# A fused attention and expert kernel: the first chunk's instructions in another order, 16 constant matmuls behind the first scores, ranks one tile later

## The chip, the cores and the metric

The kernel runs on one core of a Trainium2 chip. The metric is device time in microseconds of one execution; lower is better. TensorE (PE) does the matmuls, VectorE (DVE), ScalarE (ACT) and GpSimd (POOL) the elementwise work, SyncE (SP) issues most transfers.

## The reference

Three stages in a row: a linear attention with a decaying state, a choice of one expert for each token, and a gated feed-forward layer.

```python
B, H, S, D = 4, 8, 768, 48
for t in range(S):                                   # attention, by batch and head
    cur = einsum('bhd,bhe->bhde', u * k[t], v[t])
    y[t] = einsum('bhd,bhde->bhe', r[t], state + cur)
    state = w * state + einsum('bhd,bhe->bhde', k[t], v[t])
x = y as (3072, 384)
logits = x @ w_gate                                  # experts, 8 of them
e = argmax(logits); gate = softmax(logits)[e]; eom = sigmoid(x @ w_output_gate)[e]
x = gate * eom * (relu(x @ w1[e]) @ w2[e])
xn = x / sqrt(mean(x * x) + 1e-6) * rms_g            # feed-forward, 1536 wide
out = (silu(xn @ w_gate2) * (xn @ w_val)) @ w_out
```

## The kernel before

The attention works on 24 tiles of 128 tokens: six chunks of the sequence, in each of them the four batches. Inside a tile the recurrence is a product of r and k (by feature, `rkTb`), each multiplied by powers of w (`decayT`), under a triangular mask; from tile to tile a state `st[b]` is carried. A tile n goes through these steps:

- `decayT(n)`: VectorE multiplies the transposed r and k by the table of powers. `decayk(n)` does the same for k by token (VectorE for n < 2, GpSimd later).
- `product(n)`, `sums(n)`, `weigh(n)`: GpSimd forms r u k, VectorE sums it by head, ScalarE weighs v with it. This is the diagonal term `qv`.
- `scores(n)`: TensorE's 8 matmuls into two PSUM banks `pa` (L322), then two masks on VectorE (L324). Both buffers of the pool are used by one tile, so the next tile's scores need the masks of this one done.
- `attend(n, between)`: products of the masked scores with v into `px`, eight matmuls of 48 columns (L343) in two halves of four; in the first chunk the diagonal term is added behind them (L346, 384 columns), in later chunks it is added ahead of them (L333), with the product of r and the state (L335). Then the state's matmuls into `pkv` (L360, and L358 in later chunks) and VectorE's multiplication (L363).
- `xtrans(n)` transposes the row of outputs (L372), ScalarE copies it (L375), `logits(n)` multiplies it with the gates' weights (L383, 16 columns). `between` is called inside `attend` and holds the logits of the tile before.
- `route` works on the logits of a whole chunk. It is a generator with `yield`s, and `advance()` takes one piece of it in each tile: VectorE's choice and running counts (to L434), TensorE's ranks `prk` (L439, L440), VectorE's positions and gates (L459 to L479). `send` scatters the rows, one or two in a tile from tile 10 on.

`busy(ps, m)` issues m matmuls of constants, 128 x 512, whose result nobody reads. The table that gives their number at each place:

```python
NBUSY = (16, 8, 10, 3, 1, 1, 8)
NFILL = 6
```

TensorE, VectorE and ScalarE execute in the order in which the code is written; the order on GpSimd and SyncE is set by a scheduler, which also places the waits. The loop over n calls the steps of several tiles: with `attend(n)` come `scores(n + 1)`, `decayT(n + 2)`, `product(n + 3)` and the load of tile n + 4.

Of the kernel before, what the change touches and what calls it, by code (L numbers as in the profile page):

```python
# [39 lines left out]
NBUSY = (16, 8, 10, 3, 1, 1, 8)  # L40
# [11 lines left out]
def fused_kernel(  # L52
# [130 lines left out]
    with tc.tile_pool(name="at1", bufs=1) as at1, \  # L183
# [130 lines left out]
        def scores(n):  # L314
# [3 lines left out]
            busy(pas[0].rearrange("p a n -> p (a n)"), NBUSY[3] if n == NT - 1 else NBUSY[6] if n == 1 else NBUSY[4] if n < NFILL else 0)  # L318
# [6 lines left out]
            am[n] = a.rearrange("p g j t -> p (g j) t")  # L325

        def attend(n, between):
# [9 lines left out]
            between()  # L337
            if c < NCH - 1:
                pkv = ps1.tile([P, 512], F32, tag="kv", name=f"pkv_{n}")
            for h in range(H):  # L340
                if h == H // 2 and n < NFILL:
                    busy(pkv, NBUSY[5])
                nc.tensor.matmul(px[:, h * D:(h + 1) * D], am[n][:, h, :], vv[:, h * D:(h + 1) * D],  # L343
                                 start=(c == 0 and h == 0), stop=(c > 0), skip_group_check=True)
            if c == 0:
                nc.tensor.matmul(px[:, :DM], ident, qv.pop(n), start=False, stop=True, skip_group_check=True)  # L346
            if 1 < n + 1 < NT:
                weigh(n + 1)
            if b == 0:
# [3 lines left out]
            if c < NCH - 1:  # L353
                s = st[b] if c > 0 else at1.tile([PP, G, PD], F32, name=f"s{b}")
                sf = s.rearrange("p g e -> p (g e)")
                if c > 0:

                    nc.tensor.matmul(pkv[:PP, :DM], ident[:PP, :PP], sf, start=True, stop=False, skip_group_check=True)  # L358
                for g in range(G):
                    nc.tensor.matmul(pkv[:PP, g * PD:(g + 1) * PD],  # L360
                                     kd[n].rearrange("p h d -> p (h d)")[:, g * 2 * HP:g * 2 * HP + PP],
                                     vv[:, g * PD:(g + 1) * PD], start=(c == 0), stop=True, skip_group_check=True)
                nc.vector.tensor_tensor(sf, pkv[:PP, :DM], w128.rearrange("p g e -> p (g e)"), op=ALU.mult)  # L363
                st[b] = s
# [26 lines left out]
        def route(c, b0, b1):  # L391
# [43 lines left out]
            yield  # L435

# [81 lines left out]
        decayT(1)  # L518
# [6 lines left out]
        scores(0)  # L525

        nc.vector.tensor_tensor(pw[:, 7, :], pw[:, 6, :], pw[:, 6, :], op=ALU.mult)
        w128 = at1.tile([PP, G, PD], F32, name="w128")
# [7 lines left out]
        nc.vector.memset(cum, 0.0)  # L536

        for n in range(-3, NT + 1):
# [4 lines left out]
            if 0 <= n + 3 < NT:  # L543
                if n != -2:
# [4 lines left out]
            if n == 0:  # L549
                decayT(n + 2)  # L550
# [615 lines left out]
```

## Time and profile before

| | us |
|---|---|
| median of three runs | 923.24 |
| lowest, highest | 922.04, 928.17 |
| profiled execution | 925.68 |
| its span, first to last instruction | 923.9 |
| TensorE busy in it | 892.5 (97%) |
| mean granted clock of TensorE | 0.972 of full speed |

The span is 1.8 us shorter than the time of the same execution. A line of the timeline gives the start, the time, the engine, the line of the code, the operation with its tiles and shapes, the number of instructions that it merges, and in brackets the idle time of that engine before it with what ended it. Matmuls of 32-bit data are recorded twice, so eight of them read x16.

### The profile page before, as it was taken

The page shows a single profiled execution, that of the slowest core. Times are in us where ns is not written, and L with a number is a line of the kernel's source. Part 1 is how long each engine was busy: PE and PEld are TensorE (multiplying, and loading weights), DVE is VectorE, ACT ScalarE, POOL GpSimd, SP SyncE. Part 2 cuts the span into 40 slices and gives each one's busy share as a digit, 9 for nine tenths or more (in the row PEclk, how much of TensorE's full clock was granted, in tenths as well). Part 3 has the DMA queues.
Part 4 walks back from the last instruction along what each step waited for, and adds up shares of the span by engine and source line. Part 5 has one row for each costly group of instructions (what it writes and reads, how often), then busy time and mean ns, then how long its engine had stood idle before and what let it go on. Part 6 is the DMA issues. An engine that isn't in the chain of part 4 may idle for free.

```text
span 923.9 us, 12722 instructions
## 1 busy us (share of the span) xinstructions
PE 892.5 (97%) x4912; PEld 783.3 (85%) x4912; DVE 505.1 (55%) x887; ACT 350.8 (38%) x742; POOL 278.5 (30%) x250
## 2 busy tenths in 40 slices
PE   7899999979999999999999999999999999999997
PEld 4788888848999999998878778888888888888886
DVE  6457798755677777877579843422432242233102
ACT  1435546544444544455443422322322142241211
POOL 6446697630000000103312132132123123124121
PEclk8789979988999999999999999999999999999999
DMA  6579866444675566533321000000000000000000
GB/s 181 156 234 284 252 198 198 137 154 131 203 244 180 188 203 209 178 126 104 137 69 50 19 35 1 1 16 19 0 1 35 1 1 35 1 0 35 1 1 34
DMA packets 34263, 93.55 MB, mean 101 GB/s; under 512 B 4368, under 2 KB 12584, under 8 KB 34200
## 3 DMA queue, kind: packets, MB, share of 16 engines
q1 hardware_dynamic: 23976, 53.53, 18.9%
q0 software_dynamic: 8928, 33.83, 11.4%
q10 hardware_dynamic: 1296, 5.35, 1.5%
q8 instruction: 39, 0.64, 0.3%
q14 instruction: 24, 0.20, 0.1%
HBM read 73.19 MB, written 19.50 MB: 100 GB/s over the span
## 4 chain that ended last, share of the span: by engine, by line
PE 80%; DVE 9%; issue 4%; ACT 3%; DMA 2%; POOL 1%; SPq 0%; POOLq 0%; DVEq 0%; ACTq 0%
PE ph L955 11%; PE px L343 5%; PE p2o L619 4%; PE p2o L617 4%; PE p2o L618 4%; PE pg L618 4%; PE pv L619 4%; PE pv L617 4%; PE pv L618 4%; PE pg L619 4%; PE pg L617 4%; PE po L617 4%; PE po L618 4%; PE po L619 4%; PE pa L322 3%
## 5 line engine op out<-in xcount | busy, mean ns | idle before, releaser
L1061 POOL TENSOR_TENSOR l<-sg,h 128x512 fp32r<-128x512 f32 x69 | 92.2, 1336 | 305.2 <-ACT h L1060 303.8
L1051 DVE TENSOR_TENSOR sg<-sg,pv 128x512 f32<-128x512 f32 x72 | 49.4, 686 | 236.7 <-PE pv L619 224.2
L619 PE MATMUL p2o<-hi_o,l 128*128 128x384 f32 x276 | 93.4, 338 | 3.2 <-POOL l L1061 3.2
L1050 ACT ACTIVATE sg<-pg 128x512 f32<-128x512 f32 x72 | 42.9, 596 | 139.7 <-PE pg L619 137.4
L617 PE MATMUL p2o<-hi_o,h 128*128 128x384 f32 x276 | 93.2, 338 | 1.3 <-ACT h L1060 1.3
L618 PE MATMUL p2o<-lo_o,h 128*128 128x384 f32 x276 | 92.7, 336 | 0.0
L1060 ACT CAST h<-sg 128x512 fp32r<-128x512 f32 x69 | 42.9, 621 | 130.7 <-DVE sg L1051 130.7
L617 PE MATMUL pv<-nh,hi_v 128*128 128x512 f32 x216 | 85.3, 395 | 0.9 <-ACT sg L1050 0.9
L618 PE MATMUL pg<-nl,hi_g 128*128 128x512 f32 x216 | 85.1, 394 | 0.5 <-DVE nl L904 0.5
L619 PE MATMUL pv<-nh,lo_v 128*128 128x512 f32 x216 | 85.2, 395 | 0.0
L618 PE MATMUL pv<-nl,hi_v 128*128 128x512 f32 x216 | 85.2, 395 | 0.0
L617 PE MATMUL pg<-nh,hi_g 128*128 128x512 f32 x216 | 85.2, 394 | 0.0
L619 PE MATMUL pg<-nh,lo_g 128*128 128x512 f32 x216 | 85.1, 394 | 0.0
L120 POOL DMA_DIRECT2D raw_w<-in_w_dram x25 | 19.0, 760 | 180.9 <-DVE hl L957 83.7
L955 PE MATMUL ph<-xh,hi_w 128*128 128x432 f32 x192 | 70.3, 366 | 1.8 <-DVE hl L957 1.4
L955 PE MATMUL ph<-xh,lo_w 128*128 128x432 f32 x192 | 69.8, 364 | 0.0
L955 PE MATMUL ph<-xl,hi_w 128*128 128x432 f32 x192 | 69.5, 364 | 0.0
L617 PE MATMUL po<-hh,hi_w 128*128 128x432 f32 x192 | 69.5, 362 | 0.0
L619 PE MATMUL po<-hh,lo_w 128*128 128x432 f32 x192 | 68.8, 358 | 0.0
L618 PE MATMUL po<-hl,hi_w 128*128 128x432 f32 x192 | 68.8, 358 | 0.0
L137 DVE TENSOR_TENSOR lo_w<-raw_w,hi_w 128x768 fp32r<-128x768 f32 x54 | 49.3, 955 | 19.9 <-ACT hi_w L133 19.9
L617 PEld LDWEIGHTS p2o<-hi_o,h 128*128 128x128 f32 x276 | 51.8, 188 | 5.3 <-ACT h L1060 2.1
(208 smaller groups left out, 1890.7 us busy)
## 6 DMA issues: line engine op xcount, KB each, us to landing
raw_w<-in_w_dram POOLq DMA_DIRECT2D x25, 768.0 KB, 5.4
rkTb<-in_rkt_dram SPq DMA_DIRECT2D x48, 192.0 KB
rk<-in_rkv_dram SPq DMA_DIRECT2D x24, 384.0 KB
raw_w<-in_w_dram SPq DMA_DIRECT2D x7, 768.0 KB
xs<-zt ACTq DMA_DIRECT2D x6, 770.0 KB
v<-in_rkv_dram SPq DMA_DIRECT2D x24, 192.0 KB
craw_g<-in_m2g_dram SPq DMA_DIRECT2D x9, 512.0 KB
craw_v<-in_m2v_dram SPq DMA_DIRECT2D x9, 512.0 KB
```

What stands on the lines that cost most here:

```text
L120: ld = self.queue.dma_start(raw.rearrange("p (a n) -> p a n", a=src.shape[1]), src)
L137: eng.tensor_tensor(lo[:, t], raw[:, t], hi[:, t].bitcast(F32), op=ALU.subtract)
L322: nc.tensor.matmul(pas[j][:, g, :], kT[n][t, g, :], rT[n][t, g, :], start=True, stop=True)
L343: nc.tensor.matmul(px[:, h * D:(h + 1) * D], am[n][:, h, :], vv[:, h * D:(h + 1) * D], start=(c == 0 and h == 0), stop=(c > 0), skip_group ...
L617: nc.tensor.matmul(ps, a[0], b[0], start=first, stop=False)
L618: nc.tensor.matmul(ps, a[0], b[1], start=False, stop=False)
L619: nc.tensor.matmul(ps, a[1], b[0], start=False, stop=last)
L955: nc.tensor.matmul(ph[:, :CAP], wp[:, o:o + P], xp[:, i, :CAP], start=(j == 0), stop=(j == len(parts) - 1))
L1050: nc.scalar.activation(sg, pg, AF.Silu)
L1051: nc.vector.tensor_tensor(sg, sg, pv, op=ALU.mult)
L1060: nc.scalar.copy(hh, sg)
L1061: (nc.vector if kept else nc.gpsimd).tensor_tensor(hl, sg, hh.bitcast(F32), op=ALU.subtract)
```

## The change

At the head, tile 0's masks and tile 0's decayed k go ahead of tile 1's decay on VectorE, and the constants that stood ahead of the scores of tiles 0 and 1 become 16 constant matmuls behind the scores of tile 0. In the first chunk `between`, with the logits of the tile before, moves from ahead of the products with v to between their two halves. Tile 0's state matmuls go ahead of its diagonal term; the transposes of tile 0 go ahead of tile 2's scores, with four constant matmuls behind them. In `route` the ranks of the first four chunks come one tile later by another `yield`. The rest of the diff moves the state's steps into a function of their own.

```diff
@@ -37,7 +37,7 @@
 
 
 
-NBUSY = (16, 8, 10, 3, 1, 1, 8)
+NBUSY = (16, 8, 10, 3, 1, 1, 16, 4)
 NFILL = 6
 NCOL = NTOK + CAP
 LEAST = 1.125 * 2.0 ** -15
@@ -315,7 +315,7 @@
 
             a = at2.tile([P, G, 2, P], F32, tag="am", name=f"am_{n}")
             pas = [ps2.tile([P, G, P], F32, tag="at", name=f"pa_{n}_{j}") for j in range(2)]
-            busy(pas[0].rearrange("p a n -> p (a n)"), NBUSY[3] if n == NT - 1 else NBUSY[6] if n == 1 else NBUSY[4] if n < NFILL else 0)
+            busy(pas[0].rearrange("p a n -> p (a n)"), NBUSY[3] if n == NT - 1 else NBUSY[4] if 1 < n < NFILL else 0)
             for g in range(G):
                 for j in range(2):
                     t = slice(j * HP, j * HP + D)
@@ -324,6 +324,23 @@
                 nc.vector.tensor_tensor(a[:, :, j, :], pas[j], bcast(smask.unsqueeze(1), [P, G, P]), op=ALU.mult)
             am[n] = a.rearrange("p g j t -> p (g j) t")
 
+        pkvs = {}
+
+        def state(n):
+            c, b = divmod(n, B)
+            vv, pkv = vin[n], pkvs.pop(n)
+            s = st[b] if c > 0 else at1.tile([PP, G, PD], F32, name=f"s{b}")
+            sf = s.rearrange("p g e -> p (g e)")
+            if c > 0:
+
+                nc.tensor.matmul(pkv[:PP, :DM], ident[:PP, :PP], sf, start=True, stop=False, skip_group_check=True)
+            for g in range(G):
+                nc.tensor.matmul(pkv[:PP, g * PD:(g + 1) * PD],
+                                 kd[n].rearrange("p h d -> p (h d)")[:, g * 2 * HP:g * 2 * HP + PP],
+                                 vv[:, g * PD:(g + 1) * PD], start=(c == 0), stop=True, skip_group_check=True)
+            nc.vector.tensor_tensor(sf, pkv[:PP, :DM], w128.rearrange("p g e -> p (g e)"), op=ALU.mult)
+            st[b] = s
+
         def attend(n, between):
             c, b = divmod(n, B)
             vv = vin[n]
@@ -334,34 +351,30 @@
                 for g in range(G):
                     nc.tensor.matmul(px[:, g * PD:(g + 1) * PD], rT[n][:, g, :], st[b][:, g, :],
                                      start=False, stop=False, skip_group_check=True)
-            between()
+            if c > 0:
+                between()
             if c < NCH - 1:
-                pkv = ps1.tile([P, 512], F32, tag="kv", name=f"pkv_{n}")
+                pkv = pkvs[n] = ps1.tile([P, 512], F32, tag="kv", name=f"pkv_{n}")
             for h in range(H):
                 if h == H // 2 and n < NFILL:
                     busy(pkv, NBUSY[5])
+                if h == H // 2 and c == 0:
+                    between()
                 nc.tensor.matmul(px[:, h * D:(h + 1) * D], am[n][:, h, :], vv[:, h * D:(h + 1) * D],
                                  start=(c == 0 and h == 0), stop=(c > 0), skip_group_check=True)
-            if c == 0:
+            if c == 0 and n > 0:
                 nc.tensor.matmul(px[:, :DM], ident, qv.pop(n), start=False, stop=True, skip_group_check=True)
             if 1 < n + 1 < NT:
                 weigh(n + 1)
+            if n == 0:
+                state(n)
+                nc.tensor.matmul(px[:, :DM], ident, qv.pop(n), start=False, stop=True, skip_group_check=True)
             if b == 0:
                 xt[c] = unit("xu", f"x_{c}").rearrange("p (b d) -> p b d", b=B)
                 nc.scalar.copy(xt[c][:, :, DM:], tokid[:, c * B:(c + 1) * B].unsqueeze(2))
             nc.scalar.copy(xt[c][:, b, :DM], px[:, :DM])
-            if c < NCH - 1:
-                s = st[b] if c > 0 else at1.tile([PP, G, PD], F32, name=f"s{b}")
-                sf = s.rearrange("p g e -> p (g e)")
-                if c > 0:
-
-                    nc.tensor.matmul(pkv[:PP, :DM], ident[:PP, :PP], sf, start=True, stop=False, skip_group_check=True)
-                for g in range(G):
-                    nc.tensor.matmul(pkv[:PP, g * PD:(g + 1) * PD],
-                                     kd[n].rearrange("p h d -> p (h d)")[:, g * 2 * HP:g * 2 * HP + PP],
-                                     vv[:, g * PD:(g + 1) * PD], start=(c == 0), stop=True, skip_group_check=True)
-                nc.vector.tensor_tensor(sf, pkv[:PP, :DM], w128.rearrange("p g e -> p (g e)"), op=ALU.mult)
-                st[b] = s
+            if 0 < n < NT - B:
+                state(n)
 
         xTt = {}
 
@@ -433,6 +446,8 @@
             tk = tokid[:, n0:n0 + nb]
             V.tensor_tensor(m2, m2, tk, op=ALU.subtract)
             yield
+            if n0 < NT - 2 * B:
+                yield
 
             pr = ps1.tile([P, 512], F32, tag="sm", name=f"prk_{n0}")
             prb = pr[:, :nb * E].rearrange("p (b e) -> p b e", b=nb)
@@ -515,16 +530,16 @@
         first = decayT(0)
         loadT(2)
         loadT(3)
-        decayT(1)
         pt = ps2.tile([P, 512], F32, tag="xT", name="pt")
         for g in range(G):
             nc.tensor.transpose(pt[:, g * PP:(g + 1) * PP], fw[:, g, :], ident[:PP, :PP])
         for j in range(2):
             nc.scalar.copy(ftab.rearrange("p (g j) d -> p g j d", g=G)[:, :, j, :],
                            pt[:, :G * PP].rearrange("p (g d) -> p g d", g=G)[:, :, j * HP:j * HP + D])
+
+        nc.vector.tensor_tensor(pw[:, 7, :], pw[:, 6, :], pw[:, 6, :], op=ALU.mult)
         scores(0)
-
-        nc.vector.tensor_tensor(pw[:, 7, :], pw[:, 6, :], pw[:, 6, :], op=ALU.mult)
+        busy(ps1.tile([P, 512], F32, tag="sm", name="busy2"), NBUSY[6])
         w128 = at1.tile([PP, G, PD], F32, name="w128")
         for j in range(2):
             nc.vector.tensor_tensor(w128[:, :, j * D:(j + 1) * D],
@@ -534,6 +549,8 @@
         nc.vector.tensor_scalar(iota8, rowi[:, 0:E], -1.0, float(E), op0=ALU.mult, op1=ALU.add)
         cum = at1.tile([P, E], BF16, name="cum0")
         nc.vector.memset(cum, 0.0)
+        decayk(0)
+        decayT(1)
 
         for n in range(-3, NT + 1):
             if 0 < n + 4 < NT and n + 4 > 1:
@@ -541,16 +558,22 @@
 
             late = NT - 3 <= n < NT
             if 0 <= n + 3 < NT:
-                if n != -2:
+                if n >= -1:
                     decayk(n + 3)
                 product(n + 3)
             if n == -2:
                 sums(0)
-            if n == 0:
-                decayT(n + 2)
+            if n == 1:
+                xtrans(0)
+                weigh(1)
+                busy(ps1.tile([P, 512], F32, tag="sm", name="busy3"), NBUSY[7])
             if 0 < n + 1 < NT:
                 scores(n + 1)
-            if 0 <= n - 1 and not late:
+            if n == 0:
+                sums(1)
+                decayk(1)
+                decayT(n + 2)
+            if 1 <= n - 1 and not late:
                 xtrans(n - 1)
             if 2 < n + 2 < NT:
                 decayT(n + 2)
@@ -574,10 +597,6 @@
                 xtrans(n - 1)
             if late or n not in range(NT):
                 route_on()
-            if n == 0:
-                sums(1)
-                weigh(1)
-                decayk(1)
             if 1 < n + 2 < NT:
                 sums(n + 2)
             if NT - 4 <= n < NT:
```

VectorE at the head of the first chunk, from tile 0's decay on. `rkTb_111` and `rkTb_112` are the keys of tiles 0 and 1, `am_213` tile 0's masked scores, `w` the state's factors. Before:

```order
L309 TENSOR_TENSOR rkTb_111<-rkTb_111,decays 112x1024
L309 TENSOR_TENSOR rkTb_112<-rkTb_112,decays 112x1024
L324 TENSOR_TENSOR am_213<-pa_0_214,smask 128x4x128
L324 TENSOR_TENSOR am_213<-pa_1_215,smask 128x4x128
L527 TENSOR_TENSOR pw<-pw 112x4
L530 TENSOR_TENSOR w_228<-pw,hm 112x4x48 x2
L534 TENSOR_SCALAR iota_231<-rowi 128x8
L536 MEMSET cum_233 128x4
L281 TENSOR_TENSOR kdb_188<-rk_146,ftab 128x8x48
```

After the change:

```order
L309 TENSOR_TENSOR rkTb_111<-rkTb_111,decays 112x1024
L540 TENSOR_TENSOR pw<-pw 112x4
L324 TENSOR_TENSOR am_213<-pa_0_214,smask 128x4x128
L324 TENSOR_TENSOR am_213<-pa_1_215,smask 128x4x128
L545 TENSOR_TENSOR w_243<-pw,hm 112x4x48 x2
L549 TENSOR_SCALAR iota_246<-rowi 128x8
L551 MEMSET cum_248 128x4
L281 TENSOR_TENSOR kdb_188<-rk_146,ftab 128x8x48
L309 TENSOR_TENSOR rkTb_112<-rkTb_112,decays 112x1024
```

Tile 1's decay has gone from right behind tile 0's to behind tile 0's masks, the factors and the decayed k.

TensorE, third tile (n = 2): transposes and logits of the tile before, products with v, diagonal term and state. Before:

```order
L372 MATMUL pxT_420<-ident,x_309 128x128 x3
L383 MATMUL pxT_420<-wr,xT_424 128x16 x3
L343 MATMUL px_427<-v_241,am_340 128x48 x4
L99 LDWEIGHTS ones
L99 MATMUL pkv_434<-ones 128x512
L343 MATMUL px_427<-v_241,am_340 128x48 x4
L346 MATMUL px_427<-qv_380,ident 128x384
L360 MATMUL pkv_434<-v_241,kdb_190 112x96 x4
```

After the change:

```order
L385 MATMUL pxT_433<-ident,x_326 128x128 x3
L363 MATMUL px_440<-v_257,am_359 128x48 x4
L99 LDWEIGHTS ones
L99 MATMUL pkv_441<-ones 128x512
L396 MATMUL pxT_433<-wr,xT_437 128x16 x3
L363 MATMUL px_440<-v_257,am_359 128x48 x4
L366 MATMUL px_440<-qv_393,ident 128x384
L338 MATMUL pkv_441<-v_257,kdb_190 112x96 x4
```

The logits (`pxT<-wr`) have moved behind the first four products and the constant matmul.

TensorE around the ranks of the third chunk (n = 13 before). Before:

```order
L372 MATMUL pxT_1407<-ident,x_1270 128x128 x3
L333 MATMUL px_1414<-qv_1360,ident 128x384
L335 MATMUL px_1414<-s_455,rkTb_113 128x96 x4
L439 LDWEIGHTS ones
L439 MATMUL prk_1420<-cums_1321,ones 128x32
L440 LDWEIGHTS ltri
L440 MATMUL prk_1420<-ohb_1333,ltri 128x32
L383 MATMUL pxT_1407<-wr,xT_1411 128x16 x3
L343 MATMUL px_1414<-v_1042,am_1295 128x48 x8
```

After the change, the same tile, n = 13:

```order
L385 MATMUL pxT_1420<-ident,x_1283 128x128 x3
L350 MATMUL px_1427<-qv_1373,ident 128x384
L352 MATMUL px_1427<-s_468,rkTb_113 128x96 x4
L396 MATMUL pxT_1420<-wr,xT_1424 128x16 x3
L363 MATMUL px_1427<-v_1055,am_1308 128x48 x8
L336 MATMUL pkv_1439<-s_468,ident 112x384
L338 MATMUL pkv_1439<-v_1055,kdb_192 112x96 x4
```

And the tile behind it, n = 14:

```order
L385 MATMUL pxT_1491<-ident,x_1283 128x128 x3
L350 MATMUL px_1498<-qv_1448,ident 128x384
L352 MATMUL px_1498<-s_535,rkTb_114 128x96 x4
L454 LDWEIGHTS ones
L454 MATMUL prk_1504<-cums_1334,ones 128x32
L455 LDWEIGHTS ltri
L455 MATMUL prk_1504<-ohb_1346,ltri 128x32
L396 MATMUL pxT_1491<-wr,xT_1495 128x16 x3
L363 MATMUL px_1498<-v_1129,am_1407 128x48 x8
```

The ranks (`prk`) have moved from ahead of the logits of tile 12 to ahead of those of tile 13.

## Rows read from the trace of the kernel before

**Rows 1.** windows: stretch; busy us (instructions) of PE, PEld, DVE, ACT, POOL; PEclk; DMA share; GB/s

```profile
28.68:32.20 3.52, 3.52 (x15) 2.37 (x16) 0.82 (x2) 0.56 (x2) 2.23 (x3) 0.52 0.04 13
...
35.60:42.40 6.80, 6.80 (x33) 5.51 (x34) 1.05 (x3) 1.89 (x8) 1.35 (x2) 0.50 0.23 66
...
52.60:125.00 72.40, 72.40 (x633) 64.25 (x632) 56.40 (x110) 38.41 (x138) 45.78 (x39) 1.00 0.82 249
...
127.80:138.00 10.20, 10.20 (x49) 8.54 (x49) 8.54 (x10) 3.36 (x11) 9.22 (x9) 0.50 0.78 242
```

**Rows 2.** timeline of PE in the first chunk: start, us, line, operation, idle before

```profile
13.57 3.57 PE L99 MATMUL pa<-ones 128*128 128x512 bf16 x8 [3.48 <-DVE am L324]
...
25.88 0.84 PE L383 MATMUL pxT<-wr,xT 128*128 128x16 f32 x6 [1.63 <-ACT xT L375]
...
44.07 0.84 PE L383 MATMUL pxT<-wr,xT 128*128 128x16 f32 x6 [0.62 <-ACT xT L375]
```

**Rows 3.** timeline of DVE at the start, same columns

```profile
11.69 1.23 DVE L309 TENSOR_TENSOR rkTb<-rkTb,decays 112x1024 f32<-112x1024 f32 x1 [2.82 <-DMA rkTb<-in_rkt_dram]
12.84 1.28 DVE L324 TENSOR_TENSOR am<-pa,smask 128x512 f32<-128x512 f32 x2
...
14.78 1.43 DVE L530 TENSOR_TENSOR w<-pw,hm 112x192 f32<-112x192 f32 x2
16.13 0.16 DVE L534 TENSOR_SCALAR iota<-rowi 128x8 f32<-128x8 f32 x1
16.22 0.55 DVE L281 TENSOR_TENSOR kdb<-rk,ftab 128x384 f32<-128x384 f32 x1
```

**Rows 4.** chain that ended last, first 70 us: start, us, engine, tile, line, count

```profile
20.98 0.71 PE px L346 x2
...
50.57 0.43 PE pa L99
...
54.90 0.60 PE pxT L383 x6
55.50 0.92 PE px L343 x8
56.42 0.22 PE pkv L99
56.63 0.82 PE px L343 x8
...
58.16 0.77 PE pkv L360 x8
58.93 1.09 PE pa L322 x16
60.02 0.48 PE pxT L372 x3
```

**Rows 5.** timeline of ACT in the first chunk

```profile
17.26 1.91 ACT L302 ACTIVATE qv<-v,q 128x48 f32<-128x48 f32 x8 [8.74 <-DVE q L293]
...
21.73 0.48 ACT L352 COPY x<-px 128x384 f32<-128x384 f32 x1 [2.47 <-PE px L346]
```

**Rows 6.** timeline of POOL in the first chunk

```profile
20.25 1.00 POOL L288 TENSOR_TENSOR ru<-ru,rk 128x384 f32<-128x384 f32 x1
```

**Rows 7.** timeline of PE around the ranks of the third chunk

```profile
113.45 0.86 PE L358 MATMUL pkv<-s,ident 112*112 112x384 f32 x2
...
120.42 0.86 PE L358 MATMUL pkv<-s,ident 112*112 112x384 f32 x2
...
125.92 0.18 PE L439 MATMUL prk<-cums,ones 128*128 128x32 bf16 x1 [0.78 <-DVE cums L427]
...
129.06 1.59 PE L358 MATMUL pkv<-s,ident 112*112 112x384 f32 x2
...
140.26 0.86 PE L358 MATMUL pkv<-s,ident 112*112 112x384 f32 x2
```

**Rows 8.** timeline of DVE ahead of those ranks

```profile
120.65 3.80 DVE L425 TENSOR_TENSOR ohb<-oh,m 128x32 bf16<-128x32 f32 x1
```

## Prediction

> **What bounds the kernel now.** I read the granted clock of stretches first, then TensorE's timeline and the chain of waits in the first chunk, then what the other engines do where TensorE stands idle. The change touches only the first stage (24 tiles), so the question is what TensorE loses there.
>
> In the windows the clock has two levels, full (1.00, 2.4 GHz) and half (0.50, 1.2 GHz). In the first chunk it falls to half from 28.7 to 32.2 us and from 35.6 to 42.4 us, and once more for as long as the second time, while TensorE is busy throughout [rows 1]. From 52.6 to 125 us it never falls [rows 1]. What precedes each fall is on TensorE's timeline: logits that wait for ScalarE's copy of the transposed row, 1.63 us idle at 25.9 and 0.62 us at 44.1 us, with one more such wait between them [rows 2]. Each is followed by narrow matmuls, and the clock drops two to three microseconds later. Before the first of them there is 3.48 us of idle time, ended by the mask of tile 0 [rows 2]; VectorE did tile 1's decay (11.69 us, held by its DMA) before that mask [rows 3]. So TensorE is the bound, and in the first chunk it is slowed by short waits and by the clock that falls after them. The chain of waits gives the end of this chunk: the fourth tile's state matmuls end at 50.57 us [rows 4].
>
> Later there is one place of the same kind: the ranks of the third chunk wait 0.78 us for VectorE's running counts [rows 7], because one small VectorE operation took 3.80 us [rows 8], and from 127.8 to 138 us the clock is at half [rows 1].
>
> **The change part by part.** The sum is made against the profiled execution, 925.68 us. The median of the three other runs is 923.24 us, 2.44 lower; their spread (922.04 to 928.17) is as wide as one or two falls of the clock.
>
> *Head, VectorE.* Scores of tile 0 end at 13.57 - 3.48 = 10.09 us [rows 2]. Then VectorE does two masks (1.28), the state factors (1.43), the small table (0.16), tile 0's decayed k (0.55) and tile 1's decay (1.23) [rows 3]: 4.65 us, to 14.74 us. Tile 1's transfer has landed at 11.69 us [rows 3], so nothing else holds this decay.
>
> *Head, TensorE.* 16 constant matmuls at 0.22 us [rows 4] run from 10.09 to 13.61 us, where TensorE stood still; they cost nothing while the decay takes longer, and would cost 0.22 us each if it did not. A gap of 1.13 us is left. I take the full clock after it: the nearest row is the wait of 1.63 us at 25.9 us, through which the clock held, to fall only behind the narrow matmuls that followed [rows 1, 2]; here scores follow. If the clock falls for one spell as short as the first one in the windows (3.5 us), that costs 1.8 us.
>
> *Tile 0.* Scores of tile 1 at 1.09 us [rows 4] end at 15.83. Products with v, 0.92 and 0.82, and one constant matmul, 0.22: 17.79. State matmuls 0.77: 18.56. The diagonal term 0.71: 19.27 [all rows 4]. Its operand takes ScalarE 1.91 us [rows 5] after the sums of tile 0, which now stand behind the decay at 14.7 us, so it is there at about 17.2, in time. The copy of the row takes ScalarE 0.48 us [rows 5]: 19.75; transposes 0.48 [rows 4]: 20.23. That copy is a wait of 0.5 us on TensorE which stays. Five constant matmuls (four of them new on this path) take 1.10: 21.33; scores of tile 2: 22.42. Tile 2's sums stand ahead of its mask on VectorE and need GpSimd's product, which ended at 21.25 us before [rows 6]; that is earlier than these scores.
>
> *Tiles 1 to 3.* Between the transposes and the logits there is now the first half of the products and a constant matmul, 1.14 us, against 0.48 us for a copy of this size [rows 4, 5]: the wait goes. Products 0.92, constant 0.22, logits 0.60, products 0.82, diagonal 0.71, state 0.77 make 4.04 us [rows 4]. Tile 1 ends at 26.46 us; the next two, each with a constant, scores and transposes (0.22, 1.09, 0.48), take 5.83, to 38.12 us. Before, this was 50.57 us. The first chunk gives **12.45 us**.
>
> *Other queues.* SyncE's loads of r and k of tile 3 wait for tile 0's decayed k, which ends earlier than before, and the halves of later key transfers are issued among the r, k and v loads. Those transfers are needed two tiles (11 us) later. ScalarE's logits copy now comes behind the weighing; nothing but the routing of the chunk four tiles later reads it. These I cost at nothing; the rival with late transfers says what they cost otherwise.
>
> *Ranks a tile later.* The starts of the state matmuls are one tile apart: 120.42 - 113.45 = 6.97 us undisturbed, then 8.64 and 11.20 us [rows 7]. The excess is 1.67 + 4.23 = **5.90 us**, the wait and the half clock. One tile more is nearly twice the 3.80 us of the slow operation, so the ranks find their counts. What is late next is the mask of the tile behind the routing group on VectorE, which then comes about as its successor's scores need the banks: some tenths. Bounds: 0 (a wait moves elsewhere and the clock falls all the same) and 5.90; I take 5.90, because the wait of 0.78 us is the only idle time in those rows. Later steps of routing and the scatters move by a tile as well; scatters of the fourth chunk are issued at tile 20 as before, so the end of the stage does not move with them.
>
> *Sum.* 925.68 - 12.45 - 5.90 = **907.33 us**. From the stage's end on, TensorE has the same work and the same waits, so what is won is kept.
>
> One rule speaks against the first term. The Trainium skill, "TensorE: Matmul & The Clock Gate", section "Why this matters for your kernels", only warns of idle gaps that are longer than any between these tiles; its section "A second HAM failure mode: psum-queue depth-cycling" tells of short pauses between groups that suffice. By the first, 0.6 us of waiting is not the cause, and closing it would give no clock back; by the second it would. The trace sides with the second so far as falls follow gaps of 0.6 us, but cannot tell the gap from the narrow matmuls behind it.
>
> **The rivals.** *A: the clock falls in these tiles as before.* The narrow rows, not the wait, may let it fall. For it: a tile of the first chunk has fewer wide matmuls than a later one, and the tiles that hold the clock are all later ones [rows 1]. Against it: the later tiles have the same narrow rows, back to back, and never fall. If the spells stay, 3.5 us once and 6.8 us twice [rows 1], half of each is lost: 1.75 + 3.4 + 3.4 = 8.5, and the time is 915.8 us.
>
> *B: the ranks' term is nil.* VectorE's slow operation comes in another place, or the clock falls for another reason there. 913.2 us. For it: among the chunks whose ranks move, this one alone had such a wait, so it may belong to this execution, and others may lose elsewhere. Against it: a tile is long beside any wait in these rows.
>
> *A and B together*, or the change reordering without effect: 921.7 us, within 1%.
>
> *C: slower, through late transfers.* The first chunk goes through its tiles in 5.83 us in place of 8 to 10, so the loads have less time to get ahead, and from 52.6 to 125 us the DMA engines are at a share of 0.82 [rows 1]. If GpSimd's products come late, the sums ahead of the masks on VectorE hold those masks, TensorE waits, and the clock falls: each such stall costs 5.9 us by the ranks' rows [rows 7]. It decides from the fifth stall on: 907.3 + 5 x 5.9 = 936.8 us. Against it: TensorE does not wait once in those 72 us [rows 1].
>
> **How the numbers follow.** Forecast (904 to 911 us) 0.55, A 0.16, B 0.15, A and B 0.07, C 0.04, others 0.03. The predicted time is the forecast's, 907.3. Low end: another spell of half clock, after 158 us, may go too, some 2 us, and VectorE's operations overlap by tenths, so 903.5. High end: it takes in B and A with a microsecond of other waits, 917; above it lie A with B, and C. One per cent, about what a measurement of this kernel can tell from no change, is 9.2 us, so faster means below 914.0: the forecast, two thirds of B and a quarter of A, 0.70. Slower is C, 0.04. The same: the rest, 0.26.
>
> **What would show it.** Right: state matmuls of the fourth tile end near 38 us; no idle time between transposes and logits; a clock of 1.00 from about 14 us to past 150 us; ranks with no wait. Wrong: half-clock spells between 20 and 40 us with TensorE busy (A); a spell near 115 us (B); TensorE waiting for masks or diagonal terms in the second or third chunk (C).

## The result, and the profile after

| | before | after |
|---|---|---|
| median, us (6 runs each, taken together) | 922.64 | 913.07 |
| lowest, highest | 917.32, 930.23 | 907.31, 918.05 |
| profiled execution | 925.68 | 907.31 |
| its span, mean granted clock | 923.9, 0.972 | 905.5, 0.991 |

The ratio of the times is 0.9891, with a 95% interval of 0.9845 to 0.9937: faster, by 1.1%. The median lies inside the range, but 5.7 us above the forecast and outside the band that the forecast names (904 to 911 us); it is the time of rival B, 913.2 us. The profiled execution hit the forecast to the tenth, but it is the lowest of its six, so that agreement is luck.

Four stretches of each trace show where the time of the profiled pair went. The columns are those of [rows 1]. Before:

```profile
12.00:60.00 48.00, 43.61 (x290) 34.67 (x289) 23.56 (x38) 16.65 (x64) 23.26 (x22) 0.75 0.59 175
60.00:150.00 90.00, 89.22 (x742) 78.90 (x741) 72.10 (x143) 46.53 (x165) 63.16 (x53) 0.94 0.78 236
150.00:220.00 70.00, 61.27 (x439) 50.81 (x440) 45.87 (x151) 34.55 (x112) 33.14 (x29) 0.88 0.52 162
220.00:900.00 680.00, 672.69 (x3321) 599.58 (x3320) 349.71 (x514) 247.94 (x392) 148.20 (x126) 1.00 0.22 73
```

And after:

```profile
12.00:60.00 48.00, 45.75 (x394) 38.61 (x393) 36.78 (x55) 22.72 (x89) 34.33 (x28) 1.00 0.79 237
60.00:150.00 90.00, 89.82 (x794) 79.92 (x792) 78.03 (x147) 49.23 (x176) 70.60 (x60) 1.00 0.79 241
150.00:220.00 70.00, 61.03 (x394) 52.20 (x393) 46.49 (x149) 34.88 (x93) 20.84 (x20) 0.90 0.51 164
220.00:900.00 680.00, 671.80 (x3304) 597.42 (x3302) 342.11 (x500) 241.18 (x382) 148.24 (x126) 1.00 0.21 68
```

The granted clock is the whole story: (1 - clock) x length gives 12.0, 5.4 and 8.4 us lost before and 0, 0 and 7.0 after, a difference of 18.8 us for 18.4 us of time. TensorE's busy share is 97% in both kernels, since a slowed matmul counts as busy.

The same reckoning works for every timed execution, because each comes with its span and mean clock: **clock loss** = (1 - clock) x span. The means, like the ratios, leave out executions more than 1.5% above their kernel's fastest, which lost most to the clock (12 of the 73 of before, and of the experiments below three of number 8 and one each of numbers 2 and 6); the row of before pools all its executions beside the experiments.

| kernel | runs | time | clock loss | time less loss |
|---|---|---|---|---|
| before | 61 | 923.9 | 24.9 | 899.0 |
| after | 6 | 912.9 | 13.4 | 899.6 |

Apart from its clock the changed kernel is no faster at all; 11.5 us less are lost to the clock. Within one kernel too the spread is clock loss: 8.1 to 18.3 us in the six executions of after, whose time less loss agrees within 2 us.

TensorE's first chunk after the change, with the columns of [rows 2]:

```profile
10.18 3.63 PE L99 MATMUL busy<-ones 128*128 128x512 bf16 x16
15.49 1.26 PE L322 MATMUL pa<-rkTb 48*128 48x128 f32 x16 [1.68 <-issue]
...
20.88 0.55 PE L385 MATMUL pxT<-ident,x 128*128 128x128 f32 x3 [0.57 <-ACT x L375]
21.26 1.03 PE L99 MATMUL busy<-ones 128*128 128x512 bf16 x4
...
24.67 0.74 PE L396 MATMUL pxT<-wr,xT 128*128 128x16 f32 x6
...
27.65 0.38 PE L99 MATMUL pa<-ones 128*128 128x512 bf16 x1
...
33.46 0.38 PE L99 MATMUL pa<-ones 128*128 128x512 bf16 x1
...
36.29 0.74 PE L396 MATMUL pxT<-wr,xT 128*128 128x16 f32 x6
...
39.27 0.38 PE L99 MATMUL pa<-ones 128*128 128x512 bf16 x1
```

No logits wait any more, and the constant behind the fourth tile's state matmuls begins at 39.27 us, against 50.57 [rows 4]. From tile to tile it is 5.81 us, against 5.83 forecast. What came otherwise is the head: the gap behind the 16 constants is 1.68 us, not 1.13, and is put down to "issue", but it ends with tile 1's decay on VectorE:

```profile
10.28 1.29 DVE L324 TENSOR_TENSOR am<-pa,smask 128x512 f32<-128x512 f32 x2 [1.17 <-PE pa L322]
11.48 1.42 DVE L545 TENSOR_TENSOR w<-pw,hm 112x192 f32<-112x192 f32 x2
...
13.38 2.01 DVE L309 TENSOR_TENSOR rkTb<-rkTb,decays 112x1024 f32<-112x1024 f32 x1
```

Masks and factors took what the sum has for them (1.28 and 1.43); the decay takes 2.01 us where it took 1.23 [rows 3]. The ranks of the third chunk do not wait in this profile:

```profile
119.78 0.18 PE L454 MATMUL prk<-cums,ones 128*128 128x32 bf16 x1
```

What is left of the clock loss stands at the stage's end, as before the change. There TensorE waits for the last chunk's counts and for the gathered rows:

```profile
178.60 0.19 PE L454 MATMUL prk<-cums,ones 128*128 128x16 bf16 x1 [1.58 <-DVE cums L440]
...
180.34 0.17 PE L622 MATMUL pn<-ncum,ones 128*128 128x8 bf16 x1 [1.51 <-DVE ncum L464]
180.36 3.25 PE L99 MATMUL busy<-ones 128*128 128x512 bf16 x8
...
190.43 0.95 PE L935 MATMUL pt<-ident,xg 108*128 108x108 f32 x4 [3.56 <-DMA xg<-xs]
```

### The profile page after: what moved, and what is told of

The parts are those of the page before. It is cut to its first block, busy times and chain, and to the rows that moved or that the text cites. A ratio compares the mean times of both kernels' runs of the same rounds, so it can differ in the third digit from the quotient of the medians.

```text
span 905.5 us, 12749 instructions
## 1 busy us (share of the span) xinstructions
PE 877.8 (97%) x4923; PEld 772.4 (85%) x4923; DVE 512.9 (57%) x887; ACT 350.0 (39%) x742; POOL 282.6 (31%) x250
## 4 chain that ended last, share of the span: by engine, by line
PE 82%; DVE 8%; issue 4%; ACT 3%; DMA 2%; POOL 1%; POOLq 0%; SPq 0%; DVEq 0%; ACTq 0%
PE ph L974 12%; PE px L363 5%; PE p2o L638 4%; PE p2o L636 4%; PE p2o L637 4%; PE pg L637 4%; PE pv L638 4%; PE pv L636 4%; PE pv L637 4%; PE pg L638 4%; PE pg L636 4%; PE po L636 4%; PE po L637 4%; PE po L638 4%; PE pa L322 3%
```

## The experiments

Theory: the gain is clock, given back because TensorE's waits in the first chunk are gone. Rivals: the ranks carry part of it; the head does; the clock falls over narrow matmuls whatever the waits. Means are reckoned as above; the ratio is to the kernel before, run beside each.

| experiment | runs | ratio, 95% interval | time | clock loss | time less loss |
|---|---|---|---|---|---|
| 1 after, ranks as before | 6 | 0.9899 (0.9851, 0.9946) | 911.5 | 12.9 | 898.6 |
| 2 after, logits ahead | 11 | 0.9932 (0.9900, 0.9964) | 916.1 | 15.3 | 900.8 |
| 3 after, old head | 12 | 0.9899 (0.9872, 0.9925) | 912.8 | 14.7 | 898.1 |
| 4 after, three constants | 9 | 0.9907 (0.9872, 0.9941) | 912.9 | 12.6 | 900.3 |
| 5 before, ranks later | 12 | 1.0011 (0.9979, 1.0042) | 925.2 | 25.8 | 899.4 |
| 6 before, logits between | 5 | 0.9881 (0.9826, 0.9937) | 914.5 | 16.4 | 898.1 |
| 7 after, tile 1's decay second | 6 | 0.9843 (0.9801, 0.9884) | 912.1 | 12.7 | 899.3 |
| 8 the same, tile 0 as the others | 9 | 0.9911 (0.9870, 0.9952) | 919.0 | 21.8 | 897.2 |
| 9 after, stage's end filled | 4 | 0.9863 (0.9801, 0.9925) | 909.9 | 6.8 | 903.1 |
| 10 before, waits filled in place | 10 | 0.9901 (0.9863, 0.9938) | 914.5 | 15.1 | 899.4 |
| 11 as 8, with the four constants | 4 | 0.9891 (0.9822, 0.9960) | 912.6 | 12.8 | 899.9 |
| 12 as 9, constants moved | 6 | 0.9887 (0.9832, 0.9942) | 915.4 | 13.7 | 901.7 |

The kernel before was not equally fast beside all of them (means of 922.3 to 925.2 us), so ratios of different lines differ by some tenths of a per cent for that alone. The times of one kernel scatter with a standard deviation of 2 to 5 us, so two of these means are told apart only from about 4 us on.

**1 and 5: the ranks, taken out and alone.** Number 1 takes the added `yield` out of the changed kernel; number 5 puts it alone into the kernel before:

```diff
             V.tensor_tensor(m2, m2, tk, op=ALU.subtract)
             yield
+            if n0 < NT - 2 * B:
+                yield
```

> The changed kernel without the added yield: ranks where they stood before, all else as changed. Clock loss of a run is (1 - mean granted clock) x span; the changed kernel's six runs lose 7 to 18 us so, and less their loss they all stand at 898.6 to 900.6 us. Theory (the ranks' wait and the spell of half clock behind it are worth up to 5.9 us where they occur): median 914 to 919 us, and in the profile a wait of ranks for running counts among the first four chunks, followed by a spell of half clock. Rival B of the prediction (that wait belonged to one execution): median within 1.5 us of the changed kernel's 913, no such wait in the profile.

> The kernel before with the added yield alone. Before, 26 runs have a mean of 923.1 us, a mean clock loss of 24.6 us and 898.6 us less their loss. Theory after the first four runs (the ranks' wait is rare, and its 5.9 us belonged to the profiled execution): mean 921 to 924.5 us, loss 22.5 to 26, no wait of ranks among the first four chunks. Rival (the ranks' wait occurs in most executions of the kernel before, and only the changed kernel does without it): mean 917 to 919 us, loss 18 to 20.

Both show that the ranks are worth nothing: without the later ranks the time stays (911.5 against 912.9), and with them alone it stays too (ratio 1.0011). The slow operation of VectorE [rows 8] is not in every execution: in number 1, where the ranks stand as before, it took 0.19 us,

```profile
111.52 0.19 DVE L438 TENSOR_TENSOR ohb<-oh,m 128x32 bf16<-128x32 f32 x1
```

and its windows around the place show the full clock:

```profile
14.00:125.00 111.00, 109.56 (x954) 95.52 (x953) 89.92 (x154) 58.58 (x215) 81.41 (x67) 1.00 0.85 249
125.00:140.00 15.00, 14.08 (x122) 12.59 (x122) 14.40 (x30) 7.68 (x28) 11.85 (x10) 1.00 0.69 211
```

But it does not belong to one execution either. The same operation of the third chunk took 3.79 us in number 5 and 3.80 us in numbers 8 and 11. In number 5 the ranks, a tile later, found their counts; the scores of the tile behind waited instead, for VectorE's decay, which stands behind the slow operation and ended at 133.06 us:

```profile
123.22 3.79 DVE L425 TENSOR_TENSOR ohb<-oh,m 128x32 bf16<-128x32 f32 x1
...
133.16 1.25 PE L322 MATMUL pa<-rkTb 48*128 48x128 f32 x16 [1.29 <-issue]
```

There the clock held. In number 8, also with the later ranks, the scores waited 1.32 us, and the clock was at half from 125.4 to 132.3 us, beginning behind a wait of 0.28 us for the state just before:

```profile
128.74 2.17 PE L322 MATMUL pa<-rkTb 48*128 48x128 f32 x16 [1.32 <-issue]
```

```profile
125.40:132.30 6.90, 5.58 (x31) 4.65 (x30) 5.64 (x9) 3.76 (x13) 6.14 (x6) 0.52 1.04 298
```

So moving the ranks does not remove this wait where it occurs; it moves it to the next instruction that needs VectorE. In all four profiles the slow operation begins while GpSimd issues a scatter and ends within 0.1 us of the end of three multiplications that GpSimd does right behind it. Before, they end at 124.39 us and the operation at 120.65 + 3.80 = 124.45 us:

```profile
120.17 1.01 POOL L498 DMA_INDIRECT xs<-x,pos  x1 [0.16 <-issue]
121.20 1.28 POOL L151 TENSOR_TENSOR lo_w<-raw_w,hi_w 128x512 fp32r<-128x512 f32 x1
122.44 1.00 POOL L281 TENSOR_TENSOR kdb<-rk,ftab 128x384 f32<-128x384 f32 x1
123.41 0.98 POOL L287 TENSOR_TENSOR ru<-rk,ub 128x384 f32<-128x384 f32 x1
```

So it looks as if GpSimd held it up; no run here tests that by itself. Which of VectorE's operations meets such a run differs from profile to profile: in number 6, with the ranks as before, it was a decay (4.62 us, from 101.10 us), the scores waited 1.81 us for it, and half clock from about 107 to 111 us followed.

**2 and 6: the logits, put back and alone.** Number 6 is this edit in the kernel before; number 2 takes it out of the changed kernel:

```diff
-            between()
+            if c > 0:
+                between()
...
             for h in range(H):
...
+                if h == H // 2 and c == 0:
+                    between()
```

> The changed kernel with the logits of the tile before ahead of all products with v in the first chunk too, as before the change; all else as changed. Theory (short waits between transposes and logits make the clock fall): two waits of 0.5 to 0.7 us return in tiles 2 and 3, one to three spells of half clock lie between 22 and 50 us in the profile, the fourth tile's state matmuls end 4 to 9 us later than the changed kernel's 39.3 us, and the median is 917 to 922 us. Rival (the head and the constants did it; these waits are harmless): the waits return, no spell, end 1 to 2 us later, median 914 to 915 us.

> The kernel before with the logits between the halves of the products in the first chunk, alone. Theory (the three waits of ScalarE's copy and the spells behind them are the larger part of the gain): loss 15 to 19 us, mean 914 to 918 us, and in the profile no wait of logits for the copy in tiles 1 to 3 and no spell from 30 to 50 us. Rival (head and tile 0 carry the gain, since the changed kernel without this part loses only 2.7 us more): loss 20 to 23 us, mean 919 to 922 us.

Alone, the move gives as much as the whole change, within the scatter (0.9881, loss 16.4 in place of some 25). TensorE's timeline of number 6 has two waits left, the old head's and a short one in tile 1. The clock falls within the first (half clock from 11.7 to 18.5 us) and not behind the second; from 20 to 107 us it is at 1.00:

```profile
13.20 3.57 PE L99 MATMUL pa<-ones 128*128 128x512 bf16 x8 [3.41 <-DVE am L324]
...
25.67 0.84 PE L386 MATMUL pxT<-wr,xT 128*128 128x16 f32 x6 [0.59 <-ACT xT L378]
```

Taken out of the changed kernel it costs only 3.2 us (916.1 against 912.9), which the scatter does not tell from nothing; the median of 916.3 us lies between the theory's 917 to 922 and the rival's 914 to 915 us. Two waits of 0.57 us come back in the profile, and the clock held through both:

```profile
16.62 1.26 PE L322 MATMUL pa<-rkTb 48*128 48x128 f32 x16 [2.88 <-issue]
...
35.86 0.84 PE L393 MATMUL pxT<-wr,xT 128*128 128x16 f32 x6 [0.57 <-ACT xT L385]
...
42.50 0.84 PE L393 MATMUL pxT<-wr,xT 128*128 128x16 f32 x6 [0.57 <-ACT xT L385]
```

Its spell of half clock, 18.7 to 28.9 us, follows the gap of 2.88 us. So the parts do not add up: the logits (number 6) and the rest of the change (number 2) each remove most of the loss by themselves. Of that rest neither the ranks (number 1) nor the head (number 3) shows any worth, which leaves the new order of tile 0 with its constants; it was not run alone (and see number 8).

**10: the waits filled in place.** Nothing is moved; three constant matmuls stand ahead of the logits of tiles 1 to 3 in the kernel before:

```diff
+            if c == 0 and n > 0:
+                busy(px, 3)
             between()
```

> The kernel before with 3 constant matmuls ahead of the logits of tiles 1 to 3, in the wait for the copy of the transposed row; nothing is moved. Theory (it was the idle time of 0.6 to 1.6 us that let the clock fall): the spells between 28 and 53 us go or are halved, as with the logits moved, median 911 to 917 us. Rival (it was the run of narrow matmuls, transposes and logits back to back, which the move of the logits split up): the clock falls as before and the constants take 2 us more, 922 to 927 us.

It speaks for idle time against narrow matmuls. Transposes and logits stand in the same order as before, with 0.66 us of constants in the idle time, and the loss falls from some 25 to 15.1 us, as with the logits moved. The constants are wide, so they also part the transposes from the logits; a filling with narrow matmuls was not tried. But in number 2 transposes, wait and logits of tiles 1 and 2 follow each other unparted, and the clock is at full: there the narrow matmuls alone did not let it fall. In the profile of number 10 one wait was longer than the constants, and a half-clock spell stands behind that one; behind the filled ones there is none:

```profile
24.02 0.81 PE L99 MATMUL px<-ones 128*128 128x512 bf16 x3
25.82 0.84 PE L385 MATMUL pxT<-wr,xT 128*128 128x16 f32 x6 [0.99 <-ACT xT L377]
...
33.38 0.81 PE L99 MATMUL px<-ones 128*128 128x512 bf16 x3
34.11 0.84 PE L385 MATMUL pxT<-wr,xT 128*128 128x16 f32 x6
```

```profile
28.20:31.60 3.40, 3.40 (x15) 2.75 (x14) 0.00 (x0) 0.98 (x4) 2.53 (x3) 0.50 0.08 29
31.60:55.00 23.40, 23.40 (x203) 19.35 (x201) 14.22 (x20) 9.99 (x37) 9.75 (x9) 1.00 0.75 239
```

**3 and 7: the head.** Number 3 gives the changed kernel the head of before (tile 1's decay ahead of tile 0's masks, eight constants ahead of tile 1's scores). Number 7 puts the decay of tile 1 between:

```diff
         scores(0)
         busy(ps1.tile([P, 512], F32, tag="sm", name="busy2"), NBUSY[6])
+        decayT(1)
         w128 = at1.tile([PP, G, PD], F32, name="w128")
...
-        decayT(1)
```

> The changed kernel with the head as before: tile 1's decay ahead of tile 0's masks, one constant matmul ahead of the first scores and eight ahead of the second, none behind the first. Theory (the head's wait of 3.5 us is followed by half clock over the constants and scores, 2 to 3 us of it in work): 3.3 us of idle time at 10 us, a spell of half clock from about 12 to 18 us, second scores start at 16.5 to 17.5 us in place of 15.5, and the median is 1 to 4 us above the changed kernel's 913. Rival (all of the head's wait was hidden, since the changed kernel's decay also waits): median within 1 us of the changed kernel's.

> The changed kernel with tile 1's decay right behind tile 0's masks on VectorE, ahead of the factors, the small table and tile 0's decayed k. In five profiles the second scores of the changed head start at 15.5 to 16.6 us and TensorE stands 1.7 to 2.9 us between the constants and them; two of the five have a spell behind it. Theory (this gap is what is left of the clock loss in the first chunk): second scores start at 13.6 to 14.5 us, gap under 0.8 us, loss 9 to 11 us, time less loss 1 to 1.5 us lower than the changed kernel's 899.6, mean 908 to 910 us. Rival (the lateness only moves on to the decayed k, the sums and the diagonal term of tile 0, for which TensorE then waits): gap gone, but 1 to 2 us of waits in tile 0, loss 12 to 14 us, mean 911 to 913 us.

Number 3 is as fast as the changed kernel (912.8) with 3.37 us of idle time back in the head, so the 16 constants and the new order there are worth nothing that shows. The theory's spell did come, at half clock from about 11 to 17.5 us, as before the change; the mean does not show it. Number 7 closes the gap, scores of tile 1 begin at 13.27 us, but what follows in tile 0 is late in its place, as its rival said, and half clock from about 20.5 to 24 us stands behind these waits:

```profile
13.27 1.16 PE L322 MATMUL pa<-rkTb 48*128 48x128 f32 x16
...
18.55 0.91 PE L371 MATMUL px<-qv,ident 128*128 128x384 f32 x2 [1.23 <-ACT qv L302]
20.04 0.55 PE L385 MATMUL pxT<-ident,x 128*128 128x128 f32 x3 [0.57 <-ACT x L375]
```

Its time of 912.1 us is the changed kernel's within the spread; that its ratio is the lowest comes with a slower kernel before beside it (925.0 on average).

**4: more constants between the halves.** Three in place of one in each tile of the first chunk:

```diff
-                    busy(pkv, NBUSY[5])
+                    busy(pkv, 3 if c == 0 else NBUSY[5])
```

> The changed kernel with three constant matmuls in place of one between the halves of the products in the first chunk: 8 more, 1.8 us at full clock. The changed kernel's runs spread from 907 to 918 us and their spread is clock loss. If the runs that lose more lose it in the first chunk (its tiles still let the clock fall in some executions): losses drop to 7 to 11 us in nearly all runs, median 909 to 912 us. Rival (they lose it elsewhere, in later chunks or at the stage's end): the spread stays, median 914 to 916 us.

No difference (912.9; losses of 9.1 to 17.4 us, not the 7 to 11 of the theory): with the waits gone the clock does not fall between these tiles, so more filling buys nothing. The one spell of its first chunk, from 17.5 to 24.4 us, follows the head's gap of 2.48 us. The price of 8 x 0.22 = 1.8 us [rows 4] is hardly to be seen (time less loss 900.3 against 899.6).

**8 and 11: tile 0's transposes and its four constants.** Number 8 is number 7 with the transposes of tile 0 behind tile 2's scores, as in the other tiles, and without the four constants; number 11 keeps the constants:

```diff
             if n == 1:
-                xtrans(0)
                 weigh(1)
-                busy(ps1.tile([P, 512], F32, tag="sm", name="busy3"), NBUSY[7])
...
-            if 1 <= n - 1 and not late:
+            if 0 <= n - 1 and not late:
                 xtrans(n - 1)
```

> The kernel of the run ahead, and also tile 0's transposes behind tile 2's scores as in the other tiles, without the four constant matmuls. Theory (a wait that other work covers needs no constants): 0.57 us of wait for the row's copy and 0.88 us of constants go, time less loss another 1.4 us lower, loss as in the run ahead, mean 906.5 to 908.5 us. Rival (the constants hold the clock through tile 1, whose other matmuls are narrow): loss 2 to 4 us higher than in the run ahead, spells between 20 and 35 us, mean 909 to 912 us.

> The changed kernel with tile 1's decay second and the transposes of tile 0 behind the scores of tile 2, but with the four constant matmuls ahead of those scores kept. Theory (the four constants hold the clock): clock loss 11 to 15 us, median 910 to 914 us. Rival (the loss came with the place of the transposes): loss 22 to 26 us as without the constants, median 920 to 924 us.

Without the four constants the time less loss is the lowest of all (897.2), and the time is 6 us longer, outside both expectations: 21.8 us are lost. Its profile has two waits there, and the half clock from 23.3 to 43.7 us:

```profile
18.95 0.91 PE L371 MATMUL px<-qv,ident 128*128 128x384 f32 x2 [1.24 <-ACT qv L302]
...
21.67 1.23 PE L322 MATMUL pa<-rkTb 48*128 48x128 f32 x16 [1.59 <-DVE rkTb L309]
```

```profile
23.30:43.70 20.40, 20.40 (x99) 17.59 (x98) 6.63 (x10) 5.92 (x22) 10.30 (x11) 0.50 0.44 121
```

With the constants kept, the second wait is 0.29 us, nothing falls before 60 us, and the loss is 12.8 us. So it is the constants and not the place of the transposes; 0.9 us of matmuls that nobody reads save some 9 us of clock loss and 6 us of time (919.0 against 912.6).

**9 and 12: the stage's end.** Seven constants ahead of the last ranks, six ahead of the last counts, and 24 in place of 10 behind the cast's wait (number 9), or 18 ahead of it and 14 behind it (number 12):

```diff
-NBUSY = (16, 8, 10, 3, 1, 1, 16, 4)
+NBUSY = (16, 8, 24, 3, 1, 1, 16, 4)
...
+            if end:
+                busy(pr, 7)
...
+        busy(pn, 6)
```

> The changed kernel with 7 constant matmuls ahead of the last ranks, 6 ahead of the last counts and 24 in place of 10 behind the stage's end, where TensorE waits 1.58, 1.51 and 3.56 us. The output is unchanged. Theory (idle time lets the clock fall, filling it holds the clock): the two spells of half clock between 176 and 197 us go, 7 us of clock loss less; profiled loss 1 to 6 us, median 904 to 908 us. Rival (the spells come from the narrow matmuls of the last tiles, or the constants at half clock outlast the wait for the gathered rows): spells stay, time 911 to 917 us.

> The changed kernel with 7 and 6 constant matmuls ahead of the last ranks and counts as in the run before it, but 18 in place of 8 ahead of the cast's wait and 14 in place of 10 behind it (24 behind it ran to 197.97 us, past the landing of the gathered rows, and the time less clock loss rose from 899.6 to 903.1 us). The output is unchanged. Theory (the constants past the landing cost the 3.5 us, the rest holds the clock): time less loss 900 us, loss about 7 us, median 905 to 908.5 us, below the changed kernel's. Rival (constants in front of the waits delay what they wait for, or the clock falls in the cast's wait again): median 909 to 914 us, no better than the changed kernel.

Number 9 has the lowest mean of all, 909.9 us with 6.8 us of loss, between its two expectations: it holds 6.6 us of clock and pays 3.5 us for it in full-clock time. The 24 constants came late, behind a wait for VectorE's cast, and ran to 197.97 us:

```profile
190.94 7.03 PE L99 MATMUL busy<-ones 128*128 128x512 bf16 x24 [3.62 <-DVE ca_g L677]
198.18 1.30 PE L938 MATMUL pt<-ident,xg 108*128 108x108 f32 x12 [0.21 <-issue]
```

Number 12, meant to keep the one without the other, missed: 915.4 us with 13.7 us of loss. Its profile has half-clock spells from 17.5 to 27.8 us, behind the gap of 2.2 us in the head, and between 106 and 158 us, none of which its edit touches, and still one at the stage's end. With four and six executions the intervals of the two overlap. That filling the stage's end is worth something is not shown, and no version here is shown to beat the changed kernel.

## Why the prediction was right, and where not

*What bounds the kernel:* right. TensorE is the bound and its clock is what changes; numbers 6 and 10 show that the waits of 0.6 to 1.6 us in tiles 1 to 3 together cost 8 to 10 us through the clock. Rival A did not come in the profiled execution: the same narrow matmuls ran at 1.00 from 12 to 150 us.

By the one section of the Trainium skill that the prediction weighed ("TensorE: Matmul & The Clock Gate", "Why this matters for your kernels"), which warns of longer gaps only, such short gaps would not matter; by the other ("A second HAM failure mode: psum-queue depth-cycling") they would. Number 10 sides with the second: 0.66 us of constants in each wait took the loss from some 25 to 15.1 us. It does not say which single gap does it: number 2 held the clock through two gaps of 0.57 us, where the prediction had a fall behind each such wait.

*The first chunk, 12.45 us:* right in kind and a little too large: 50.57 - 39.27 = 11.30 us in the profiled pair, and 11.0 us is the mean difference of the whole time. Of the missing 1.15 us, 0.75 are the head: the scores of tile 1 began at 15.49 us, not 14.74. The steps up to the end of the constants held; then the decay of tile 1 took 2.01 us for 1.23. A few tenths more were lost in tile 0. GpSimd's multiplications ran beside it and were stretched as well:

```profile
12.99 1.32 POOL L287 TENSOR_TENSOR ru<-rk,ub 128x384 f32<-128x384 f32 x1 [0.30 <-DMA rk<-in_rkv_dram]
14.38 1.86 POOL L288 TENSOR_TENSOR ru<-ru,rk 128x384 f32<-128x384 f32 x1
```

The second one takes 1.00 us undisturbed [rows 6]. In the row by which I had priced the decay [rows 3], GpSimd ran beside it too, but there the decay began first, at 11.69 us, and kept its 1.23 us; GpSimd's multiplication took twice its time:

```profile
11.79 1.99 POOL L288 TENSOR_TENSOR ru<-ru,rk 128x384 f32<-128x384 f32 x1
```

What the sum left out is which of the two comes first. The Trainium skill, "SBUF — State Buffer", section "Who interferes with whom", says that VectorE and GpSimd share one pair of ports as an exclusive lock. The rows agree: held until 14.31 us, where GpSimd's first operation ends, and then at 1.23 us, the decay would end at 15.54; it ended at 15.39.

The prediction's reading of the clock before also left out one of four spells, the one behind the head's wait of 3.48 us: eight constants took 3.57 us there [rows 2], twice the 0.22 us each of full speed. The four together are the 12.0 us lost from 12 to 60 us; rival A's 8.5 us covers three of them. And the falls came not always two to three microseconds after the logits began: 2.8, then about 1.5 and 1.8 us.

*That a gap of 1.13 us in the head does no harm:* held in the profiled execution with 1.68 us. But the wait of 1.63 us was not the nearest row for it: the head's own wait of 3.48 us was, and half clock stands behind that one. Numbers 2, 4, 9 and 12, with gaps of 2.2 to 2.9 us in the same place, each show a spell between 17 and 29 us. This is where part of the spread of the changed kernel may come from; number 7, which closes the gap, only moved the wait into tile 0 and lost as much (12.7 us).

*The ranks, 5.90 us:* this is the step that failed, and rival B was right: 0 (numbers 1 and 5). The excess in [rows 7] was real, but two steps from it to the term fail. It is not in every execution (the operation took 3.80 us here, 0.19 us in number 1). And where it is, a tile's delay of the ranks does not take the wait away: what the prediction priced at "some tenths", the lateness of what stands behind on VectorE, was 1.29 us of waiting scores in number 5 and 1.32 us in number 8. The lower bound, "a wait moves elsewhere", was the right one; the prediction took the upper because the wait was the only idle time in the rows. The profiled pair alone would have confirmed the term, since from 60 to 150 us it lost 5.4 us less.

*The sum:* 907.33 was made against one execution with 25.9 us of clock loss, close to the mean of before (24.9), so the base was fair. From it 11.3 us come off for the first chunk, not 18.35: 914.4 us, beside a measured median of 913.07. That the profiled execution of after came to 907.31 us is because it happened to lose 8.1 us, against 13.4 on average. So the range holds the median because it took rival B in, not because the sum was right.

*Rival C* did not come: in the profile after, TensorE does not wait in the second and third chunk, and time less clock loss rose by 0.6 us only, while 11 more constant matmuls in the first chunk run partly in idle time.

What stays open: why the same kernel loses 8 us in one execution and 18 in the next, and which of the gaps left sets that: in the head, at the stage's end, or where the scores of a later chunk wait behind a slow VectorE operation (numbers 6 and 8).

## What to carry to other kernels

Before a term is built on a stall, ask two things: whether it is in every execution (the row of 3.80 us was in four of fourteen profiles, while the waits of 1.63, 0.57 and 0.62 us in tiles 1 to 3 came again to the hundredth in number 5), and whether the change removes its cause or only takes one waiting instruction out of its way. Where TensorE is the bound and its clock falls, work out (1 - clock) x span for every timed run; if the time less that is the same for two kernels, only the clock differs, and a few constant matmuls in the wait can give what a reordering gives. Such filling should end before what it waits for lands: number 9's came late, and gave back 3.5 of the 6.6 us that it held.

## What the runs showed that I had not expected

- Time less clock loss is 897 to 903 us for all fourteen kernels, though waits of several microseconds were added or removed among them: at full clock there was next to nothing to win.
- Three constant matmuls in each of three waits are worth as much as the whole reordering (914.5 against 912.9 us, with overlapping intervals).
- The removal of 0.9 us of constants (number 8) cost 9 us of clock loss in the mean, and its profile shows a single spell of 20.4 us.
- One VectorE operation of the third chunk, on 128 x 32 elements, took 3.8 us in four of fourteen profiles, each time until a run of three GpSimd multiplications had ended, and 0.19 us in the other ten.
